# Attention in one kernel with a mixture of experts: the values' shared block kept twice, and transposed-weight buffers of the width of their half

## The chip, the cores and the metric

The kernel runs on one core of a Trainium2 chip. The metric is the device time in microseconds (us); lower is better. Before the change the median of three runs is 808.53 us (808.22 to 809.11).

## The reference, cut to what matters

Three layers follow each other: attention, a mixture of experts, and a feed-forward layer with a rational function. The change is in the attention, whose last line is the product of the weights and the values.

```python
B, H, S, D = q.shape                      # 2, 8, 576, 64
scores = (1 / np.sqrt(D)) * np.matmul(q, k.transpose(0, 1, 3, 2))
scores = scores + bias.transpose(2, 0, 1)[None]          # a small network of positions
attn = np.exp(scores - scores.max(-1, keepdims=True))
attn = attn / (attn.sum(-1, keepdims=True) + 1e-09)
attn_out = np.matmul(attn, v)             # the change is here
x = moe(attn_out)                         # 4 experts, 1152 tokens, 512 -> 1024 -> 512
out = rational_ffn(x)                     # 512 -> 2048 -> 512
```

## The kernel before, in words

The work runs in four stages: the bias of the positions (to about 62 us), attention (to about 217 us), the experts, and the rational layer. There is one instruction queue for each engine. TensorE is PE, VectorE DVE, ScalarE ACT, GpSimd POOL; SyncE (SP) issues nearly all transfers. In the attention stage a small planner, class `Flow`, writes the order of the instructions: each step has an assumed duration and an urgency from a table (`CFG`), and the order comes out of these alone. The change touches neither the durations nor the table.

Attention goes over eight passes n, one for each batch and pair of heads; the two heads of a pair are worked on together. A head has 576 keys, which is four and a half blocks of 128. The two halves share the ninth block: chunk 4 of the values' tile `splv` holds the last 64 keys of head 0 in partitions 0 to 63 and the first 64 keys of head 1 in partitions 64 to 127. The transposed weights lie in the same way: `pt` holds four full blocks for each head, `pe` the shared block.

Precision is kept by splitting numbers in a high and a low part: `splv` holds both side by side (128 columns), and the weights come as `pth`/`peh` (high) and `ptl`/`pel` (low).

The steps of a pass:

- `load_raw` (L517) fetches k, q and v of a pass; `split_hi` and `split_lo` (L527, L532, on POOL) split them; `qk_T` (L548, L556) transposes q and k; `swap_k` (L561) copies k with its halves swapped.
- `scores` (L594, PE), `biased` (L608, DVE), `exps` (L616, ACT), `norm` (L636, POOL).
- `transp` and `transp_rest` (L653, L666, L669, PE) transpose the normalized weights; ACT writes the high part (L678), DVE the low part (L682).
- `av` (L701, PE) multiplies with the values, once for each half of the queries (256 or 320 of them) and each head: ten matmuls, of which the first eight use 128 rows of the array. The last two, for the shared block, use the 64 rows of the head in question. A pass has four such runs of ten, so the kernel has 32.
- `other_half` (L708, ACT), `add_halves` (L714, DVE) and `x_parts` (L721, L722, POOL) bring the result to the experts' input `x`.

In the bias stage ACT makes a quarter of the hidden layers (L413) and all the results `bo` (L442). Four results share a buffer; there are two buffers, and each is stored to DRAM by SP (L431). The ninth result can't be written before the first buffer has been stored. During this stage SP also loads k, q and v of passes 0 and 1 and then eight small tables (`ab`, `dp`, L198 to L207), all in one queue.

Of the kernel before, what the change touches and what calls it, by code (L numbers as in the profile page):

```python
# [9 lines left out]
F32 = mybir.dt.float32  # L10
F32R = mybir.dt.float32r
# [7 lines left out]
B, H, S, D, HID = 2, 8, 576, 64, 32  # L19
# [5 lines left out]
P = 128  # L25
# [109 lines left out]
class Kernel:  # L135
# [366 lines left out]
    def load_raw(self, n, nm):  # L502

        if n >= 8:
            return
        nc = self.nc
        p, b = n // 2, n % 2
        src = self.t[nm][b, 2 * p:2 * p + 2]  # L510
        r = self.front.tile([P, 9, D], F32, tag="raw" + nm, bufs=1, name="raw" + nm)
        if nm == "q":
            for h in range(2):
                nc.sync.dma_start(out=r[:, 4 * h:4 * h + 4], in_=src[h, 0:512].rearrange("(c p) d -> p c d", p=P))
                nc.sync.dma_start(out=r[64 * h:64 * h + 64, 8], in_=src[h, 512:S].rearrange("(a q) d -> q a d", a=4))
        else:
            nc.sync.dma_start(out=r, in_=src.rearrange("h s d -> (h s) d").rearrange("(c p) d -> p c d", p=P))  # L517
        self.raw[n, nm] = r
# [4 lines left out]

    def split_hi(self, n, nm):
        nc, raw = self.nc, self.raw[n, nm]
        s = self.front.tile([P, 9, 2, D], F32R, tag="spl" + nm, bufs=(2 if nm == "v" else 1), name="spl" + nm)
        nc.gpsimd.tensor_scalar(out=s[:, :, 0, :], in0=raw, scalar1=1.0, scalar2=1.0, op0=ALU.mult, op1=ALU.mult)  # L527
        self.spl[n, nm] = s

# [35 lines left out]
    def attention_setup(self):  # L565

        nc, early = self.nc, self.early
# [69 lines left out]

        def pt_tiles(n, half):
            if (n, half) not in PT:
                PT[n, half] = tuple(  # L640
                    (self.att.tile([P, 4, 2, 320], F32R, tag="pt" + x, bufs=2, name="pt" + x),
                     self.att.tile([P, 320], F32R, tag="pe" + x, bufs=2, name="pe" + x)) for x in "hl")
            return PT[n, half]

        def transp(g):

            n, c, h = where(g)
            (mh, eh), (ml, el) = pt_tiles(n, 0 if c < 2 else 1)
            pt = Pt[n, c]
            o = P * (c % 2) if c < 4 else 256  # L650
            ps = self.one().rearrange("p (e i) -> p e i", e=4)
            for e in range(4):
                nc.tensor.transpose(ps[:, e, :], pt[:, 640 * h + e * P:640 * h + e * P + P], self.ident)  # L653
            if c < 4:
                todo = [(ps, mh[:, :, h, o:o + P], ml[:, :, h, o:o + P])]
            else:
                todo = [(ps.rearrange("p e (h q) -> p e h q", h=2), mh[:, :, :, 256:320], ml[:, :, :, 256:320])]
            parts[g] = (todo, [])

        def transp_rest(g):  # L660
            n, c, h = where(g)
            (mh, eh), (ml, el) = pt_tiles(n, 0 if c < 2 else 1)
            ps = self.one()
            if c < 4:
                for i in range(2):
                    nc.tensor.transpose(ps[:, P * i:P * i + P], Pt.pop((n, c - 1 + i))[:, 512:640], self.ident)  # L666
                rest = [(ps[:, 0:256], eh[:, 0:256], el[:, 0:256])]
            else:
                nc.tensor.transpose(ps[:, 0:P], Pt.pop((n, c))[:, 512:640], self.ident)  # L669
                rs = [slice(64 * hh, 64 * hh + 64) for hh in range(2)]  # L670
                rest = [(ps[r, r], eh[r, 256:320], el[r, 256:320]) for r in rs]
            parts[g] = (parts[g][0], rest)
# [14 lines left out]
        def av(n, half, h, part):  # L687
            W = 256 if half == 0 else 320
            vs = self.spl[n, "v"]
            (mh, eh), (ml, el) = PT[n, half]  # L690
            if part == 0:
                avs[n, half, h] = self.one()
            ps = avs[n, half, h]
            for e in ((0, 1), (2, 3, 4))[part]:
                for (m, el_) in ((mh, eh), (ml, el)):
                    if e < 4:
                        lh, rh = vs[:, 5 * h + e].rearrange("p a d -> p (a d)"), m[:, e, h, :W]
                    else:
                        r = slice(64 * h, 64 * h + 64)
                        lh, rh = vs[r, 4].rearrange("p a d -> p (a d)"), el_[r, :W]  # L700
                    nc.tensor.matmul(ps[:, :W], lhsT=lh, rhs=rh, start=(e == 0 and m is mh), stop=(e == 4 and m is ml))  # L701

        def other_half(n, half, h):
# [36 lines left out]
        def schedule():  # L740
# [54 lines left out]
            for n in range(8):  # L795
                p_hold = {}
                for r in range(9):
# [36 lines left out]
                    if r in (3, 8):  # L834
                        gs = range(9 * n, 9 * n + 4) if r == 3 else range(9 * n + 4, 9 * n + 9)
                        deps = [split_op[n, "v"]] + [Lop[x] for x in gs] + [Lop2[x] for x in gs if x in Lop2]
                        pre = None
                        xt = fl.hold("xt", 1)
                        adds = []
                        for h in range(2):  # L840
                            one = fl.hold("one", 4)
                            for part in range(2):
                                dur = (.48, .71)[part] if r == 3 else (.59, .88)[part]
                                lastav = h == 1 and part == 1
                                pre = fl.op("PE", dur, g + off("V", n), lambda n=n, half=half, h=h, part=part: av(n, half, h, part), deps if pre is None else [pre],
                                            take=[one] if part == 0 else [], free=[pt_hold[n, half]] if lastav else [])
                            go = fl.op("ACT", .385, g + off("G", n), lambda n=n, half=half, h=h: other_half(n, half, h), [pre] + adds, take=[xt] if h == 0 else [])
                            adds.append(fl.op("DVE", .41, g + off("G", n) + .1, lambda n=n, half=half, h=h: add_halves(n, half, h), [go], free=[one]))
                        avop.setdefault(n, []).append(pre)
                        xp[n, half] = fl.op("POOL", (1.2, 1.4)[half], g + off("X", n), lambda n=n, half=half: x_parts(n, half), adds, free=[xt])  # L850
# [433 lines left out]
```

## Time and profile before

The page describes one profiled execution.

| what | value |
|---|---|
| profiled execution, its own time | 807.95 us |
| its span, first to last instruction | 806.0 us |
| median of three runs | 808.53 us |
| PE busy | 783.1 us (97%) |
| DVE busy | 649.4 us (81%) |
| ACT busy | 488.3 us (61%) |
| POOL busy | 455.0 us (56%) |
| granted TensorE clock | 0.999 of full speed |

The engine with the largest share is PE. Shares are means over four stages with different limits, so a stage is read by itself: its stretch in the table of busy times, the chain of waits through it, and the instructions in order of time. A matmul's duration in the trace is longer than the distance between two matmuls, because they are pipelined; so costs of matmuls are read from the distances between their starts.

### The profile page before, as it was taken

The numbers are of one execution on the slowest core, as the hardware profiler recorded it, in microseconds if no ns is written. First come the engines' busy times: TensorE is split into PE (matmuls) and PEld (weight loads), VectorE is DVE, ScalarE is ACT, GpSimd is POOL, SyncE is SP. The second block draws the span as 40 slices with busy tenths as digits, with TensorE's granted clock in tenths as the row PEclk, the third lists the DMA queues.
The fourth block names the chain that finished last, engine by engine and source line by source line (L and its number), as shares of the span: only waits on it lengthen the run. The fifth ranks groups of instructions, "written<-read, shape, count | busy, mean of one in ns | idle before, by whom it ended". The sixth has DMA issues, their size and how long they took to land.

```text
span 806.0 us, 13644 instructions
## 1 busy us (share of the span) xinstructions
PE 783.1 (97%) x4980; PEld 683.0 (85%) x4980; DVE 649.4 (81%) x1183; ACT 488.3 (61%) x932; POOL 455.0 (56%) x454
## 2 busy tenths in 40 slices
PE   6888999999999999999999999999999999999997
PEld 2337899988998999999999999999889889998986
DVE  7987888888687888878889878888678667888775
ACT  5898898889443334333333433333369998887772
POOL 3167689778346555444355545345166977754442
PEclk9999999999999999999999999999999999999999
DMA  5788747491013434432444333333130311000012
GB/s 127 264 284 229 196 104 201 105 233 54 1 30 102 131 131 129 137 116 93 147 139 144 131 105 119 117 131 105 40 105 27 119 64 53 1 0 1 1 40 78
DMA packets 67634, 87.37 MB, mean 108 GB/s; under 512 B 33520, under 2 KB 42096, under 8 KB 67440
## 3 DMA queue, kind: packets, MB, share of 16 engines
q1 hardware_dynamic: 66992, 86.35, 35.4%
q8 instruction: 39, 0.64, 0.3%
q14 instruction: 27, 0.22, 0.1%
q10 hardware_dynamic: 576, 0.16, 0.1%
HBM read 60.12 MB, written 21.36 MB: 101 GB/s over the span
## 4 chain that ended last, share of the span: by engine, by line
PE 77%; ACT 7%; POOL 6%; issue 4%; DVE 4%; DMA 2%; SPq 0%; POOLq 0%; DVEq 0%; ACTq 0%
PE ps_o L900 20%; PE ps_o L1150 11%; PE ps_y L992 10%; PE ps_h L1142 10%; PE ps_x L992 8%; PE ps L701 6%; PE ps L594 5%; PE ps L653 4%; ACT hid L413 2%; ACT bo L442 2%; POOL we L303 2%; PE ps_x L890 1%; PE ps L548 1%; POOL wml L303 1%; PE ps_y L890 1%
## 5 line engine op out<-in xcount | busy, mean ns | idle before, releaser
L900 PE MATMUL ps_o<-we,hs 128*128 128x512 f32 x810 | 203.4, 392 | 0.0
L900 PEld LDWEIGHTS ps_o<-we,hs 128*128 128x128 f32 x810 | 146.1, 188 | 25.8
L303 POOL TENSOR_TENSOR we<-wstg,we 128x512 fp32r<-128x512 f32 x40 | 57.0, 1446 | 130.3 <-ACT we L297 130.3
L906 DVE SCALAR_TENSOR_TENSOR acc<-ps_o,prob,acc 128x512 f32<-128x512 f32 x135 | 99.7, 743 | 30.1 <-PE ps_o L900 29.9
L1123 POOL TENSOR_TENSOR qq<-qq,ha 128x384 f32<-128x384 f32 x48 | 48.9, 1019 | 71.0 <-ACT qq L1120 71.0
L1150 PE MATMUL ps_o<-wmh,hs 128*128 128x512 f32 x252 | 83.5, 392 | 1.1 <-POOL hs L1134 1.1
L1142 PE MATMUL ps_h<-x,wmh 128*128 128x384 f32 x288 | 73.7, 337 | 0.0
L636 POOL TENSOR_SCALAR P<-P,ri 128x576 f32<-128x576 f32 x72 | 53.0, 747 | 33.3 <-DVE ri L627 18.8
L930 ACT ACTIVATE hs<-ps_x 128x576 fp32r<-128x576 f32 x32 | 20.8, 651 | 80.7 <-DVE ps_x L1004 74.0
L608 DVE CUSTOM_DVE_ANT_0 P<-ps,bias 128x576 f32<-128x576 f32 x72 | 53.6, 750 | 14.9 <-PE ps L594 12.9
L424 PE MATMUL ps_ab<-hid,wm 128*32 128x288 f32 x576 | 47.0, 425 | 12.0 <-DVE hid L416 7.5
L616 ACT ACTIVATE P<-P,nm 128x576 f32<-128x576 f32 x72 | 56.0, 780 | 3.3 <-DVE nm L608 3.1
L1129 DVE SCALAR_TENSOR_TENSOR qq<-qq,rr 128x384 f32<-128x384 f32 x48 | 26.6, 554 | 38.1 <-ACT rr L1128 35.1
L1150 PEld LDWEIGHTS ps_o<-wmh,hs 128*128 128x128 f32 x252 | 47.3, 188 | 11.4 <-POOL hs L1134 1.9
L328 POOL TENSOR_TENSOR wu<-wt,wu 128x512 fp32r<-128x512 f32 x28 | 36.2, 1314 | 36.4 <-ACT wu L324 36.4
L1142 PEld LDWEIGHTS ps_h<-x,wmh 128*128 128x128 f32 x288 | 52.6, 188 | 2.0
L682 DVE TENSOR_TENSOR ptl<-ps,pth 128x512 fp32r<-128x512 f32 x72 | 48.5, 683 | 5.2 <-ACT pth L678 4.7
L416 DVE TENSOR_SCALAR hid<-ltab,shift 128x576 f32<-128x576 f32 x108 | 52.6, 558 | 0.0
L594 PE MATMUL ps<-kh,qs 128*128 128x288 f32 x168 | 50.3, 321 | 1.4 <-DVE nm L608 1.3
L1134 POOL TENSOR_TENSOR hs<-pp,hs 128x384 fp32r<-128x384 f32 x48 | 48.9, 1019 | 3.5 <-issue 2.8
L424 PEld LDWEIGHTS ps_ab<-hid,wm 128*32 128x32 f32 x576 | 18.4, 112 | 37.0 <-ACT bo L442 13.9
L1150 PE MATMUL ps_o<-wml,hs 128*128 128x512 f32 x126 | 49.5, 393 | 0.0
(142 smaller groups left out, 2098.9 us busy)
## 6 DMA issues: line engine op xcount, KB each, us to landing
wstg<-moe_w SPq DMA_DIRECT2D x32, 512.0 KB, 3.7
bias_d<-bo SPq DMA_DIRECT2D x9, 1152.0 KB, 5.4
bias<-bias_d SPq DMA_DIRECT2D x16, 576.0 KB, 5.1
w<-moe_w_in SPq DMA_DIRECT2D x16, 512.0 KB, 4.4
w<-moe_w_out SPq DMA_DIRECT2D x16, 512.0 KB, 3.8
kl<-kh SPq DMA_DIRECT2D x16, 288.0 KB, 4.4
w_u<-wmag SPq DMA_DIRECT2D x16, 256.0 KB, 2.4
w_d<-wmag SPq DMA_DIRECT2D x16, 256.0 KB, 2.4
```

What stands on the lines that cost most here:

```text
L303: nc.gpsimd.tensor_tensor(out=lo[:, sl], in0=stg[:, sl], in1=hi[:, sl].bitcast(F32), op=ALU.subtract)
L416: eng.tensor_scalar(out=ht, in0=d, scalar1=c, scalar2=0.0, op0=ALU.add, op1=ALU.max)
L424: nc.tensor.matmul(ps[32 * q:32 * q + 32, i, 0:288], lhsT=wm, rhs=hs[q][:, 288 * i:288 * i + 288], start=True, stop=True)
L594: nc.tensor.matmul(ps[:, half, dst:dst + w], lhsT=lhs, rhs=k[:, src:src + w], start=(i == 0), stop=(i == len(m) - 1))
L608: nc.vector.tensor_tensor_reduce(out=Pt[u][:, S * h:S * h + S].rearrange("p (a b) -> p a b", a=2), in0=ps[:, :, 0:288], in1=self.bias_t[n ...
L616: nc.scalar.activation(out=pt, in_=pt, func=AF.Exp, scale=-1.0, bias=stat.pop(g), accum_out=sums[n, c][:, h:h + 1])
L636: nc.gpsimd.tensor_scalar(out=pt[:, sl], in0=pt[:, sl], scalar1=ri, scalar2=1.0, op0=ALU.mult, op1=ALU.mult)
L900: nc.tensor.matmul(ps, lhsT=a, rhs=w[:, f, :], start=(f == i == 0), stop=(f == 1 and i == 2))
L906: nc.vector.scalar_tensor_tensor(out=acc[:, t], in0=ps, scalar=pr, in1=acc[:, t], op0=ALU.mult, op1=ALU.add)
L992: nc.tensor.matmul(ps[:, half, 0:288], lhsT=wu[:, w, i, k], rhs=x[v][:, k, 288 * half:288 * half + 288], start=(start and k == j == 0), st ...
L1142: nc.tensor.matmul(ps, lhsT=w[:, k, fo:fo + P], rhs=v[:, k, :], start=(k == i == 0), stop=(k == 3 and i == 2))
L1150: nc.tensor.matmul(ps, lhsT=a[:, P * tt:P * tt + P], rhs=w[:, f % 2, :], start=(f == i == 0), stop=(f == 3 and i == 2))
```

## The change

The raw values of a pass now have ten chunks instead of nine. Chunk 4 holds the last 64 keys of head 0, and zeros in the other 64 partitions; the new chunk 9 holds the first 64 keys of head 1, and zeros in the others. One buffer `rawv` is made in the first pass, its zeros are written once by POOL, and all passes load into it. A load of v is four transfers instead of one. The split works on ten chunks. The two matmuls of the shared block then take all 128 rows: the zeros remove the other head's keys. The transposed weights of each half of the queries get a buffer of their own with the width of that half, one of each, in place of two of the larger width.

```diff
+        if nm == "v":
+            if n == 0:
+                self.rawv = self.front.tile([P, 10, D], F32, tag="rawv", bufs=1, name="rawv")
+                for h in range(2):
+                    nc.gpsimd.memset(self.rawv[64 - 64 * h:128 - 64 * h, 4 + 5 * h], 0.0)
+            r = self.rawv
+            rows = src.rearrange("h s d -> (h s) d").rearrange("(c p) d -> p c d", p=P)
+            for h in range(2):
+                nc.sync.dma_start(out=r[:, 5 * h:5 * h + 4], in_=rows[:, 5 * h:5 * h + 4])
+                nc.sync.dma_start(out=r[64 * h:64 * h + 64, 4 + 5 * h], in_=rows[64 * h:64 * h + 64, 4])
+            self.raw[n, nm] = r
+            return
...
-        s = self.front.tile([P, 9, 2, D], F32R, tag="spl" + nm, bufs=(2 if nm == "v" else 1), name="spl" + nm)
+        s = self.front.tile([P, 9 + (nm == "v"), 2, D], F32R, tag="spl" + nm, bufs=(2 if nm == "v" else 1), name="spl" + nm)
...
+                W = (256, 320)[half]
                 PT[n, half] = tuple(
-                    (self.att.tile([P, 4, 2, 320], F32R, tag="pt" + x, bufs=2, name="pt" + x),
-                     self.att.tile([P, 320], F32R, tag="pe" + x, bufs=2, name="pe" + x)) for x in "hl")
+                    (self.att.tile([P, 4, 2, W], F32R, tag=f"pt{x}{half}", bufs=1, name="pt" + x),
+                     self.att.tile([P, W], F32R, tag=f"pe{x}{half}", bufs=1, name="pe" + x)) for x in "hl")
...
-                    if e < 4:
-                        lh, rh = vs[:, 5 * h + e].rearrange("p a d -> p (a d)"), m[:, e, h, :W]
-                    else:
-                        r = slice(64 * h, 64 * h + 64)
-                        lh, rh = vs[r, 4].rearrange("p a d -> p (a d)"), el_[r, :W]
+                    lh, rh = vs[:, 5 * h + e].rearrange("p a d -> p (a d)"), m[:, e, h, :W] if e < 4 else el_[:, :W]
                     nc.tensor.matmul(ps[:, :W], lhsT=lh, rhs=rh, start=(e == 0 and m is mh), stop=(e == 4 and m is ml))
```

The order on PE, DVE and ACT is that of before, instruction for instruction. SP's queue grows by three transfers in each of the eight loads of v. The first place is in the bias stage: the load of v for pass 1 (`rawv`), the small tables (`ab`, `dp`), and then the first stores of the bias (`bias_d`). Before:

```order
14 L515 DMA rawq<-q 64x1x64
15 L517 DMA rawv<-v 128x9x64
16 L198 DMA ab<-moe_a 128x4
17 L199 DMA ab<-moe_b 128x2
18 L207 DMA dp<-moe_domain_probs 128x4x4
19 L207 DMA dp<-moe_domain_probs 128x3x4
20 L207 DMA dp<-moe_domain_probs 64x4 x2
21 L207 DMA dp<-moe_domain_probs 64x1x4 x2
22 L431 DMA bias_d_71<-bo 128x4x576 x2
```

The same place of SP's queue with the change:

```order
17 L528 DMA rawq<-q 64x1x64
18 L520 DMA rawv<-v 128x4x64
19 L521 DMA rawv<-v 64x64
20 L520 DMA rawv<-v 128x4x64
21 L521 DMA rawv<-v 64x64
22 L198 DMA ab<-moe_a 128x4
23 L199 DMA ab<-moe_b 128x2
24 L207 DMA dp<-moe_domain_probs 128x4x4
25 L207 DMA dp<-moe_domain_probs 128x3x4
26 L207 DMA dp<-moe_domain_probs 64x4 x2
27 L207 DMA dp<-moe_domain_probs 64x1x4 x2
28 L431 DMA bias_d_71<-bo 128x4x576 x2
```

The first store of the bias stands three transfers later in the same queue. The second place is on SP in the attention stage, the copy of k (`kl`) and the load of v for pass 6, ahead of q for pass 7. Before:

```order
94 L561 DMA kl<-kh 64x1152
95 L562 DMA kl<-kh 64x1152
96 L517 DMA rawv<-v 128x9x64
97 L514 DMA rawq<-q 128x4x64
98 L515 DMA rawq<-q 64x1x64
```

The same place of SP's queue with the change:

```order
112 L574 DMA kl<-kh 64x1152
113 L575 DMA kl<-kh 64x1152
114 L520 DMA rawv<-v 128x4x64
115 L521 DMA rawv<-v 64x64
116 L520 DMA rawv<-v 128x4x64
117 L521 DMA rawv<-v 64x64
118 L527 DMA rawq<-q 128x4x64
119 L528 DMA rawq<-q 64x1x64
```

The load of q, which POOL splits, stands three transfers later.

## Rows read from the trace of the kernel before

**Rows 1.** The page, busy time of PE (us, share, instructions)
```profile
PE 783.1 (97%) x4980; PEld 683.0 (85%) x4980; DVE 649.4 (81%) x1183; ACT 488.3 (61%) x932; POOL 455.0 (56%) x454
```
**Rows 2.** Busy times of a stretch of the attention: us, PE, PEld, DVE, ACT, POOL, clock, DMA
```profile
87.00:180.70 93.70, 92.95 (x703) 84.63 (x701) 78.64 (x246) 83.14 (x207) 77.72 (x105) 1.00 0.66 169
```
**Rows 3.** Chain of waits, bias stage and attention: start us, us, what
```profile
57.96 0.64 ACT bo L442
...
80.34 0.76 POOL P L636
...
82.00 0.80 PE ps L594 x4
```
**Rows 4.** PE in order of time, 256 queries: start us, us, engine, line, tiles, shapes
```profile
133.40 0.29 PE L594 MATMUL ps<-kl,qs 128*128 128x288 f32 x1
133.53 0.28 PE L701 MATMUL ps<-pth,splv 128*128 128x256 f32 x1
...
134.35 0.28 PE L701 MATMUL ps<-ptl,splv 128*128 128x256 f32 x1
134.56 0.38 PE L701 MATMUL ps<-peh,splv 64*128 64x256 f32 x1
134.79 0.27 PE L701 MATMUL ps<-pel,splv 64*128 64x256 f32 x1
134.99 0.40 PE L594 MATMUL ps<-kh,qs 128*128 128x288 f32 x1
135.23 0.29 PE L594 MATMUL ps<-kl,qs 128*128 128x288 f32 x1
```
**Rows 5.** PE in order of time, 320 queries
```profile
105.60 0.31 PE L701 MATMUL ps<-ptl,splv 128*128 128x320 f32 x1
...
106.48 0.31 PE L701 MATMUL ps<-ptl,splv 128*128 128x320 f32 x1
106.72 0.41 PE L701 MATMUL ps<-peh,splv 64*128 64x320 f32 x1
...
107.46 0.30 PE L701 MATMUL ps<-ptl,splv 128*128 128x320 f32 x1
```
**Rows 6.** Groups by line and shape: count, busy us, mean ns
```profile
L701 PE MATMUL ps<-peh,splv 64*128 64x320 f32 x16 | 6.6, 411 | 0.0
L701 PE MATMUL ps<-peh,splv 64*128 64x256 f32 x16 | 6.1, 382 | 0.0
```
**Rows 7.** Weight loads in order of time, at the run of rows 5
```profile
106.34 0.19 PEld L701 LDWEIGHTS ps<-ptl,splv 128*128 128x128 f32 x1
106.72 0.18 PEld L701 LDWEIGHTS ps<-peh,splv 64*128 64x128 f32 x1 [0.19 <-ACT qs L556]
```
**Rows 8.** Waits of ACT, 82 to 200 us: total us, times, longest
```profile
ACT xt L708 <- PE ps L701: 6.2, 13, 0.9
```
**Rows 9.** Issues of SP in the bias stage: start us, us, line, tiles
```profile
13.77 0.55 SPq L515 DMA_DIRECT2D rawq<-q  x1
14.53 0.41 SPq L517 DMA_DIRECT2D rawv<-v  x1
14.98 0.60 SPq L198 DMA_DIRECT2D ab<-moe_a  x1
...
19.65 1.45 SPq L431 DMA_DIRECT2D bias_d<-bo  x1
```
**Rows 10.** ACT in order of time, bias stage
```profile
25.71 0.74 ACT L442 ACTIVATE bo<-ps_ab,rpsi 128x576 f32<-128x576 f32 x1 [2.58 <-DMA bias_d<-bo]
```
**Rows 11.** Groups by line and shape, POOL's split of v
```profile
L532 POOL TENSOR_TENSOR splv<-rawv,splv 128x576 fp32r<-128x576 f32 x8 | 11.5, 1435 | 0.2
L527 POOL TENSOR_SCALAR splv<-rawv 128x576 fp32r<-128x576 f32 x8 | 5.6, 702 | 0.0
```
**Rows 12.** SP's issue of the v of pass 6
```profile
158.90 0.72 SPq L517 DMA_DIRECT2D rawv<-v  x1
```
**Rows 13.** POOL in order of time, split of the q of pass 7
```profile
166.90 0.67 POOL L527 TENSOR_SCALAR splq<-rawq 128x576 fp32r<-128x576 f32 x1 [0.16 <-issue]
```

## The prediction, made before the changed kernel had run

> **What bounds the kernel now.** I read the shares of the engines first: PE is busy for 97% of the span, no other engine over 81% [rows 1]. That is a mean, so next came the stretch the change lies in. From 87.0 to 180.7 us, five of the eight attention passes, PE is busy 92.95 of 93.70 us, ACT 83.14, DVE 78.64, POOL 77.72 [rows 2]. So PE is the bound there, and ACT is second with 10.56 us free. The chain of waits says the same from the other side: until about 82 us it still runs through POOL, from 82.00 us on it is almost all PE [rows 3]. A busy share does not say that PE works well, though, so I then read the starts of the matmuls in order of time.
>
> In a run of ten with 256 queries, the eight matmuls on 128 rows start 0.117 us apart: 134.35 − 133.53 = 0.82 over seven steps [rows 4]. Then the distances grow: 0.21 to the first 64-row matmul, 0.23 to the second, 0.20 to the next instruction (again on 128 rows) and 0.24 to the one behind. With 320 queries the clean distance is (106.48 − 105.60)/6 = 0.147, and the same four steps take 107.46 − 106.48 = 0.98 us [rows 5]. The reader is to see that the two narrow matmuls, which do half the work, are late on their way in and on their way out.
>
> **The change part by part.**
>
> *The 64-row pair goes.* Without late starts the four steps would take 3 × 0.117 + 0.135 = 0.49 us with 256 queries (0.135 is the distance of the scores' matmuls, 288 wide, 0.13 between the last two ahead of the run [rows 4]) and 4 × 0.147 = 0.59 with 320. They take 0.88 and 0.98, so a pair costs 0.39 us in either width. There are 16 + 16 pairs [rows 6]. Where transposes follow instead of wide matmuls (13 of the 32, counted in the chain) I see only some 0.3 us, as the last of the four steps is hardly late: 19 × 0.39 + 13 × 0.32 = 11.6 us. The replacement runs over 128 rows with the same number of columns, so I take 0.117 and 0.147 us for it, the distance of its eight neighbours. What is taken away lies on the bounding engine, except in the first run, near 77 us, where the chain goes through POOL [rows 3]: 2 pairs, 0.78 us, cost nothing now and give nothing back. That leaves 10.8 us.
>
> The row on weight loads shows how it is lost: a normal load starts while the matmul before it still runs (106.34), but the load of the 64-row block begins at 106.72, the same moment as its matmul, after 0.19 us without a load [rows 7]. The Trainium skill, "TensorEngine Tiling (Array Packing)", section "Key Properties", says that changing the tiling mode empties the engine first. It would put the cost on the two changes, (0.09 + 0.08) × 32 = 5.4 us by this case's distances; the trace has all four steps late, so the sum stands by the trace.
>
> *What else has to keep up.* PE would gain 10.8 us over the eight passes less most of the first, say 7.2, so 1.5 us a pass. ACT has 10.56/5 = 2.1 us a pass free, so it would run at 96 to 97%. It fits, but queues in fixed order at this load lose something. For it: what ACT waits for most is this same product, 6.2 of its waits [rows 8], so ACT gains from the cure as well. I take 85% of 10.8: 9.2 us. Bounds: the 6.2 us alone, if ACT's other waits stay, and the full 10.8.
>
> *Three more transfers in each load of v.* In the bias stage SP is the late one. SP issues v of pass 1 at 14.53, the small tables from 14.98, and the first store of the bias at 19.65 without a pause in between [rows 9], so SP's queue and not ACT sets when that store leaves. The store lands, and ACT, which had to wait for it for 2.58 us, goes on at 25.71 [rows 10]. From there ACT sets the pace until 58.6 us, in the chain of waits [rows 3]. So what is added ahead of that store is on the path: three issues at 0.55 + 0.04 = 0.59 us, 1.77 us, and POOL's longer split of v of pass 0, for which the load of pass 1 waits: (0.702 + 1.435)/9 = 0.24 us [rows 11]. That makes 2.0 us. Bounds: nothing, if the store lands sooner after its issue than now, and 2.6 if the small pieces also slow the transfers behind them. I take 2.0, since the issue slots are measured. The Trainium skill, "DMA: Bandwidth & Descriptors", section "Rules for kernel authors", advises against it too: transfers to disjoint halves of the partitions should be one, many small ones should be joined. It has no price for SP's queue, and the sum goes by SP's rows.
>
> In the attention stage the loads of v have a pass or so of slack themselves. What stands behind them in SP's queue has less: the q of pass 7, issued after the v at 158.90 [rows 12], is split by POOL at 166.90 after a short wait of 0.16 us [rows 13]; it will be some 1.8 us late, and POOL's split with it. The transposes that need POOL's next results come more than 2 us after those, so I put 0.2 us for it, bounds 0 and 1.8.
>
> *Rest.* POOL's split of v grows by 0.24 us in six passes; POOL has 16 us free in rows 2, so 0. The two fills of zeros lie at the start, where POOL waits for input: 0. The narrower weight buffers are used in the same rotation, one for each half: 0; bounds ±0.5, since addresses move.
>
> **Sum.** −9.2 + 2.0 + 0.2 = −7.0 us on the profiled execution's 807.95 us (span 806.0): 800.95. The median of the runs is 0.58 above it, so 801.5 us.
>
> **The rivals.**
> 1. *ACT takes over.* PE's freed time turns into waits for ACT and DVE, and only the 6.2 us go. For it: ACT at 97% in a fixed order. Against: its free time is more than is needed. −6.2 + 2.2 = −4.0: 804.5.
> 2. *Everything is realized, and the bias stage loses nothing.* −10.8 + 0.2: 797.9. For it: PE's chain without gaps. Against: SP's unbroken row of issues ahead of the store.
> 3. *The late starts stay.* The pair might be late since it changes operands (`pe` for `pt`), not rows. The Trainium skill, "TensorE: Matmul & The Clock Gate", section "Step-by-step: what each phase is for", says that a weight load is pulled ahead of running matmuls when its row groups don't conflict or it goes to the background buffer; by it the 64-row load should not be late at all, and something else would have to be the cause. As a mechanism of this kernel: the change of operands costs, and remains. Against it: from the scores to the first product, other weights and other operands, the distance is 0.13 us, no delay [rows 4]. Result: 2.2 us slower, 810.7.
> 4. *SP's queue becomes the bound: slower.* Each of the six later loads of v holds up q, k or the bias behind it by 2.0 us, and POOL or DVE miss them. 2.0 + 6 × 2.0 − 10.8 = +3.2: 811.7. It decides from the fifth such load on, as 2.0 + 2.0 n passes 10.8 at n = 4.4. For it: the wait in rows 13. Against: the engines' rows show but that one such wait.
>
> **How the numbers follow.** My forecast, with gains of 9 to 5 us (799.5 to 803.5): 0.50. Rival 1 (803.5 to 806.9): 0.20. Rival 2 (below 799.5): 0.17. Rival 3: 0.07. Rival 4: 0.03. Gain and loss balancing: 0.03. About 0.2%, 1.6 us, is what a measurement of this kernel can tell from no change; so faster 0.87, same 0.03, slower 0.10. The range goes from the lower end of rival 2, 797.5, into rival 1, 805.8; that leaves out rivals 3 and 4, the balance and the worst of rival 1, together under 0.2. The forecast's own range is 799.5 to 803.5.
>
> **What would show it.** In the changed profile the ten matmuls of a run should start evenly, 0.117 or 0.147 us apart, and no weight load begin with its own matmul there. The first store of the bias should be issued near 21.7 us, and ACT's wait for it grow from 2.58 to about 4.6. ACT's waits for the product should shrink to below half. From the end of the attention on all stages should keep their length. I am wrong if the last two matmuls of a run stay late, if PE gets new waits for ACT, DVE or POOL of over 4 us in the attention, or if the bias stage ends at its old time.

## The result, and the profile after

The median of three runs of the changed kernel is 801.25 us (801.18 to 801.47), against 808.53 before: a ratio of 0.9909, interval 0.9894 to 0.9923. The forecast was 801.5. The profiled execution took 801.47 us (span 799.6), 6.5 less than that of before.

The page's busy times, to set beside [rows 1]:

```profile
PE 774.1 (97%) x4980; PEld 682.6 (85%) x4980; DVE 649.4 (81%) x1183; ACT 488.9 (61%) x932; POOL 445.3 (56%) x456
```

PE does the same 4980 matmuls in 9.0 us less. Five passes by the table of busy times, answering to [rows 2]:

```profile
87.00:180.70 93.70, 91.45 (x749) 89.42 (x748) 83.61 (x263) 88.96 (x220) 82.68 (x110) 1.00 0.67 173
```

In equal time PE now gets through 749 instructions instead of 703. ACT is at 95% and PE, at 98%, still ahead of it. PE in order of time, 256 queries, is what answers to [rows 4]:

```profile
131.92 0.30 PE L607 MATMUL ps<-kl,qs 128*128 128x288 f32 x1
132.05 0.28 PE L711 MATMUL ps<-pth,splv 128*128 128x256 f32 x1
...
132.88 0.28 PE L711 MATMUL ps<-ptl,splv 128*128 128x256 f32 x1
132.99 0.28 PE L711 MATMUL ps<-peh,splv 128*128 128x256 f32 x1
133.11 0.28 PE L711 MATMUL ps<-pel,splv 128*128 128x256 f32 x1
133.23 0.29 PE L607 MATMUL ps<-kh,qs 128*128 128x288 f32 x1
133.36 0.29 PE L607 MATMUL ps<-kl,qs 128*128 128x288 f32 x1
```

From the eighth matmul to the second instruction behind the run it is now 133.36 − 132.88 = 0.48 us, where [rows 4] had 0.88. The weight loads in a run with 320 queries, as in [rows 7]:

```profile
158.77 0.19 PEld L711 LDWEIGHTS ps<-ptl,splv 128*128 128x128 f32 x1
158.92 0.19 PEld L711 LDWEIGHTS ps<-peh,splv 128*128 128x128 f32 x1
159.06 0.19 PEld L711 LDWEIGHTS ps<-pel,splv 128*128 128x128 f32 x1
```

They follow each other every 0.15 us, those of the shared block as the others. ACT's wait for the product, 6.2 us in [rows 8], is small (82 to 195 us):

```profile
ACT xt L718 <- PE ps L711: 1.7, 6, 0.5
```

The price stands in the bias stage. SP's issues, from the v of pass 1 to the first store (compare [rows 9]):

```profile
14.68 0.38 SPq L520 DMA_DIRECT2D rawv<-v  x1
15.10 0.51 SPq L521 DMA_DIRECT2D rawv<-v  x1
...
16.85 0.58 SPq L198 DMA_DIRECT2D ab<-moe_a  x1
...
20.16 1.22 SPq L207 DMA_DIRECT2D dp<-moe_domain_probs  x1
...
22.11 0.53 SPq L431 DMA_DIRECT2D bias_d<-bo  x1
```

ACT's wait for that store ([rows 10]):

```profile
27.05 0.74 ACT L442 ACTIVATE bo<-ps_ab,rpsi 128x576 f32<-128x576 f32 x1 [3.35 <-DMA bias_d<-bo]
```

The store is issued 2.46 us later, but from its issue to ACT's going on it is 27.05 − 22.11 = 4.94 us instead of 6.06, so ACT loses 1.34. Most of that difference is SP's own time for the issue, 1.45 us in [rows 9] and 0.53 here; from the end of the issue to ACT's going on it is 4.61 us before and 4.41 after. A long issue now stands at one of the small tables instead (1.22 us, at 20.16).

Last, POOL's split of the q of pass 7 ([rows 13]), and the group of its waits:

```profile
164.11 0.68 POOL L540 TENSOR_SCALAR splq<-rawq 128x576 fp32r<-128x576 f32 x1 [0.94 <-DMA rawq<-q]
```

To find where time goes I set the same instruction's start in both traces side by side. The first product stands at 76.47 us before and 79.15 after; two lines show the other end, the first matmul of the experts, before and after:

```profile
218.26 2.01 PE L890 MATMUL ps_x<-x,we 128*128 128x288 f32 x14
```
```profile
212.03 3.46 PE L900 MATMUL ps_x<-x,we 128*128 128x288 f32 x24
```

| point | before | after | difference |
|---|---|---|---|
| last product of the bias stage | 61.24 | 62.60 | +1.36 |
| first product with the values | 76.47 | 79.15 | +2.68 |
| pass 1 | 95.97 | 97.63 | +1.66 |
| pass 5, its second run | 172.95 | 168.10 | −4.85 |
| pass 5, its third run | 180.67 | 176.60 | −4.07 |
| experts' first matmul | 218.26 | 212.03 | −6.23 |
| span | 805.95 | 799.62 | −6.33 |

The reader is to see three things: a loss of 1.36 in the bias stage; a further 1.3 us lost from 62.6 to 79.2 that no term of the forecast holds; and a gain of 8.9 us from there to the experts, in which 0.8 is given back at pass 5. That unforeseen 1.3 is a fall of TensorE's granted clock. The table of busy times there (clock third from the end), and PE's rows:

```profile
66.20:69.70 3.50, 3.50 (x19) 3.48 (x19) 1.30 (x3) 1.81 (x5) 3.50 (x5) 0.51 0.84 258
```
```profile
66.12 0.96 PE L561 MATMUL ps<-identr,splk 128*128 128x128 f32 x6 [2.17 <-ACT bo L442]
...
67.25 0.44 PE L607 MATMUL ps<-kl,qs 128*128 128x288 f32 x1
67.49 0.44 PE L607 MATMUL ps<-kh,qs 128*128 128x288 f32 x1
...
69.85 0.29 PE L607 MATMUL ps<-kl,qs 128*128 128x288 f32 x1
69.98 0.29 PE L607 MATMUL ps<-kh,qs 128*128 128x288 f32 x1
```

After a wait of 2.17 us for ACT the scores' matmuls start 0.24 us apart, at 1.2 GHz, until 69.63; then 0.13, at 2.4 GHz. The trace of before has the same wait of 2.17 us, and no fall:

```profile
64.76 0.71 PE L548 MATMUL ps<-identr,splk 128*128 128x128 f32 x6 [2.17 <-ACT bo L442]
...
65.51 0.29 PE L594 MATMUL ps<-kl,qs 128*128 128x288 f32 x1
65.64 0.29 PE L594 MATMUL ps<-kh,qs 128*128 128x288 f32 x1
```

Whether the change brings it was open.

### The profile page after: what moved, and what is told of

Same layout as the page of the kernel before. It is cut to its first block, busy times and chain, and to the rows that moved or that the text cites. A ratio compares the mean times of both kernels' runs of the same rounds, so it can differ in the third digit from the quotient of the medians.

```text
span 799.6 us, 13676 instructions
## 1 busy us (share of the span) xinstructions
PE 774.1 (97%) x4980; PEld 682.6 (85%) x4980; DVE 649.4 (81%) x1183; ACT 488.9 (61%) x932; POOL 445.3 (56%) x456
## 4 chain that ended last, share of the span: by engine, by line
PE 78%; ACT 10%; POOL 5%; DVE 4%; issue 2%; DMA 1%; SPq 0%; POOLq 0%; DVEq 0%; ACTq 0%
PE ps_o L910 23%; PE ps_y L1002 11%; PE ps_o L1160 10%; PE ps_h L1152 9%; PE ps_x L1002 8%; PE ps L607 4%; PE ps L711 4%; PE ps L667 3%; ACT bo L442 2%; ACT hid L413 2%; ACT P L629 1%; POOL wml L303 1%; PE ps_x L900 1%; PE ps L561 1%; POOL we L303 1%
```

## The experiments

The ratios are against runs of the kernel before on the same chip (medians 807.97 and 807.98 in the first two sessions, 807.59 and 808.25 beside e9 and e10).

**e1, the loads alone.** The changed kernel, with the 64-row pair as before:

```diff
+                    if e < 4:
+                        lh, rh = vs[:, 5 * h + e]..., m[:, e, h, :W]
+                    else:
+                        r = slice(64 * h, 64 * h + 64)
+                        lh, rh = vs[r, 4 + 5 * h]..., el_[r, :W]
```

> The changed kernel's loads, split and buffers, but the two matmuls of the shared block on 64 rows as before (the right half of chunks 4 and 9). Theory A (the gain is the 64-row pair's late starts, the loads cost): slower than before by 1.3 us, ACT's longer wait for the first bias store, or by up to 2.7 us if the TensorE clock falls once near 66 us as it did with the change: 809.8 to 811.2 us. All 32 pairs keep their late starts of 0.39 us. Rival B (buffers and loads bring the gain): 801 to 805 us.

810.19 us, ratio 1.0027 (1.0017 to 1.0037): the loads cost, and pay nothing. The bias stage ends 1.63 us late, ACT's wait for the store is 3.9 us. The first product comes 2.89 us late; the 1.3 in between are the fall again (its clock is at 1.2 GHz from 66.3 to 69.7). From there to the end the distance stays at 2.8 to 2.9, so six later loads of v cost nothing while the product is slow, and ACT's wait for the product is the old 6.2.

**e2, the wide pair alone.** The kernel before, with two slices changed:

```diff
-                        lh, rh = vs[r, 4]..., el_[r, :W]
+                        lh, rh = vs[:, 4]..., el_[:, :W]
```

> The kernel before, with all 128 rows for the two matmuls of the shared block; the other head's 64 keys are left in the sum instead of zeros, nothing else differs. Theory A: the ten matmuls of a run start evenly, 0.117 and 0.147 us apart, ACT's wait for the first bias store stays 2.58 us, and the time falls by 8.9 us (what the changed kernel gained between its first product and the end of the attention) to 10.8 us: 797.7 to 799.6 us. Rival B (the pair is late since its operands change): 808.5 us, the pairs still late.

798.30 us, 0.9878 (0.9865 to 0.9892). PE with 320 queries:

```profile
121.63 0.31 PE L700 MATMUL ps<-ptl,splv 128*128 128x320 f32 x1
121.78 0.31 PE L700 MATMUL ps<-peh,splv 128*128 128x320 f32 x1
121.92 0.31 PE L700 MATMUL ps<-pel,splv 128*128 128x320 f32 x1
122.07 0.31 PE L700 MATMUL ps<-pth,splv 128*128 128x320 f32 x1
```

Same operands, same order, and the delay is gone: it belongs to the number of rows. From the start of the first run of ten to the start of the last the gain is 9.6 us; the later experiments are compared by the same measure. By the medians e1 loses 2.2 us and e2 gains 9.7, together −7.5, where the change has −7.3.

**e4, the small tables behind the first store.** The changed kernel, with the tables' loads two steps later:

```diff
-            if gg == 3:
+            if gg == 5:
                 self.setup_const()
```

> The changed kernel, with the small tables (ab, dp) issued behind the first bias store instead of ahead of it. Theory A (SP's queue delays the store, ACT waits for it): the store is issued near 18 us instead of 22.1, ACT's wait of 3.35 us falls under 0.5, and the bias stage ends some 3 us sooner: 798.0 to 798.6 us; 1.3 us less still if the TensorE clock no longer falls near 66 us. Rival (the store's landing is set by the transfers in flight, not by its issue): within 0.5 us of 801.25.

798.59 us, 0.9883 (0.9868 to 0.9898). The store's issue:

```profile
17.66 0.38 SPq L431 DMA_DIRECT2D bias_d<-bo  x1
```

ACT has no wait for it any more, and the bias stage ends at 59.81, 2.8 us sooner than in the changed kernel: the loss of that stage was SP's queue. Pass 5 still gives back 0.85 us, with POOL's wait for the q of pass 7 at 1.02.

**e5, the same in the kernel before.**

> The kernel before, with the small tables (ab, dp) issued behind the first bias store. Theory A (SP's queue, not the change's loads, set when the store left in the kernel before as well): ACT's wait of 2.58 us is gone, the bias stage ends 1.5 to 2.6 us sooner, the time is 1.5 to 2.6 us below that of the kernel before on the same chip. Rival (the store waits for something else): within 0.5 us of the kernel before.

806.59 us, 0.9983 (0.9975 to 0.9992): 1.4 us, short of the least expected. The bias stage ends 1.73 us sooner, as theory A has it, but the first product only 0.60, since the profiled execution has the fall of the clock:

```profile
64.20:67.60 3.40, 3.40 (x16) 3.38 (x16) 1.98 (x5) 2.33 (x6) 3.40 (x5) 0.50 0.94 209
```

So the fall also comes in a kernel without the change.

**e6, PE kept busy in its wait.** The changed kernel with 24 matmuls, whose results nobody reads, at the end of the bias stage:

```diff
+        ps = self.ps.tile([P, 2, 512], F32, tag="ab", bufs=3, name="ps_ab")
+        for i in range(6):
+            for q in range(4):
+                nc.tensor.matmul(ps[32 * q:32 * q + 32, i % 2, 0:288], lhsT=wm, rhs=hids[:, q, 0:288], start=True, stop=True)
```

> The changed kernel, with 24 more matmuls at the end of the bias stage, into a spare bank that nothing reads, so that PE works through most of its wait of 2.2 us at 64 us. Theory A (that wait lets the TensorE clock fall to 1.2 GHz from 66.2 to 69.6 us, which costs 1.3 us): no stretch at 1.2 GHz there, the first product of pass 0 starts some 1.3 us sooner than 79.15, the time is 799.6 to 800.2 us. Rival (the fall belongs to something else in the stretch): the stretch stays, or moves, and the time is 801.0 to 801.6 us.

800.52 us, 0.9906 (0.9890 to 0.9921). In its profile the clock does not fall, but the first product comes at 79.00, only 0.15 sooner: the added matmuls run until 66.5 and take what the clock gives. Inconclusive on the price of the fall. The profile shows something else, though: e6 has the changed kernel's attention unaltered, yet POOL does not wait for the q of pass 7, pass 5 gives nothing back, and the attention gains 9.4 us, where the changed kernel gains 8.4.

```profile
162.93 0.68 POOL L544 TENSOR_SCALAR splq<-rawq 128x576 fp32r<-128x576 f32 x1
```

SP spends 0.55 to 0.59 us on each of the four issues of that q here; in the changed kernel's profile one of the four takes 1.19.

**e10, the changed kernel again.** After e5 and e6 I looked at the mean granted clock of every single execution, and put the question to the unaltered kernel.

> The changed kernel itself, unaltered, executed more often. What it tells apart: whether the fall of TensorE's granted clock near 66 us in its profile belongs to the kernel or to the single execution. The kernel before, in the 34 executions beside the earlier experiments, had a mean granted clock of 0.999 in 16, with 806.56 to 807.98 us, and of 0.997 to 0.998 in 18, with 807.97 to 809.48; the profiled execution had 0.999 and no fall, the changed kernel's 0.998 and one fall. Theory A (each execution has the fall or not, whatever the kernel, and it costs about 1.1 us): the changed kernel's executions fall into two groups as well, 0.999 with 799.7 to 800.5 us and 0.996 to 0.998 with 800.8 to 801.8. Theory B (the changed bias stage brings the fall): all of them have 0.998 or less and 800.8 to 801.8 us, none 0.999.

(The count in it is off by one: 17 and 17 of the 34.) Four executions: 800.04 and 800.46 us with a clock of 1.000, 801.09 and 801.36 with 0.997. That is theory A; B falls. The profiled one is that with 800.04; the same stretch of PE, same wait, no fall:

```profile
65.90 0.71 PE L561 MATMUL ps<-identr,splk 128*128 128x128 f32 x6 [2.17 <-ACT bo L442]
66.44 0.36 PE L607 MATMUL ps<-kh,qs 128*128 128x288 f32 x1
66.65 0.29 PE L607 MATMUL ps<-kl,qs 128*128 128x288 f32 x1
66.77 0.29 PE L607 MATMUL ps<-kh,qs 128*128 128x288 f32 x1
```

Its bias stage ends 1.14 us late, its first product stands at 77.60 (+1.13), so nothing is lost in between, and the experts begin at 210.47:

```profile
210.47 1.74 PE L900 MATMUL ps_x<-x,we 128*128 128x288 f32 x11
```

That is −7.79 against before, the span 798.2 against 805.95. With the 7 runs beside this one the kernel before has 41 executions with a known clock: 19 at 0.999 with a median of 807.52 us, 22 at 0.997 or 0.998 with 808.73. Read so, about half of the executions have a fall, and it costs about 1 us in either kernel. For executions without a profile the mean is a sign and no proof, since it also counts the end of the span: e4's profile has 0.998 without such a fall, as its last 2.44 us, in which no engine computes, are at 1.2 GHz.

**e7, two raw buffers.** e4 with two buffers for the raw v, so that v is loaded a pass earlier and q stands ahead of it:

```diff
-                self.rawv = ...(bufs=1)
+                self.rawv = [...(bufs=2) for _ in range(2)]
...
+            if gg == 7:
+                self.load_v(2)
```

> The kernel with the tables later, with two buffers for the raw v, each loaded a pass earlier, and the loads of v for passes 5 and 7 issued behind the q that follows them in SP's queue. Order on PE, DVE, ACT and POOL unchanged. Theory A (the q of pass 7 comes late because the four transfers of v stand ahead of it; that cost 0.9 to 1.2 us near 171 us): POOL's wait for that q falls from 0.9 us to 0, the time is 0.8 to 1.3 us below that of the kernel with the tables later alone: 797.3 to 797.8 us. Rival (from pass 5 on ACT is full, and the time would be lost later): within 0.4 us of 798.59.

800.63 us, 0.9906 (0.9892 to 0.9921): a miss. I had put the load of pass 2 ahead of the second store of the bias, and repeated the fault that e4 had mended:

```profile
33.61 0.74 ACT L443 ACTIVATE bo<-ps_ab,rpsi 128x576 f32<-128x576 f32 x1 [3.61 <-DMA bias_d<-bo]
```

The bias stage ends 2.29 us late, and the first product comes 3.34 late, with the clock at 1.2 GHz from 68.5 to 71.9. From the first run of ten to the last, though, this kernel gains 9.4 us where e4 gains 8.4, and POOL's wait for q is gone.

**e9, that load behind the store.** e7 with `gg == 9` in place of `gg == 7`.

> The kernel of e7_two_raw_buffers with one change: the load of v of pass 2 is issued at step 9 of the bias stage instead of step 7, so behind the second store of the bias in SP's queue instead of ahead of it. Theory A (the second raw buffer saves the late q of pass 7, and e7 lost its time only since that load stood ahead of a store): ACT's wait of 3.6 us for the store goes, the bias stage ends at e4_tables_later's -1.4 us against before, and the attention gains e7's 9.4 us from the first product on instead of e4's 8.4: 798.59 less 0.8 to 1.3, so 797.3 to 797.8. POOL's wait for q of pass 7 (1.02 us in e4) is gone. Theory B (the gain of e7 in the attention was only the lateness of its bias stage being caught up): the attention gains 8.4 as in e4, 798.4 to 798.8. A fall of the granted clock between 62 and 72 us, which some of these kernels show and others not, would put either 0.9 to 1.3 us higher.

798.20 us (796.53 to 798.77), 0.9878 (0.9858 to 0.9898). ACT does not wait, the bias stage ends at −1.48, the attention gains 9.4 by the same measure, POOL does not wait for q: theory A in each step, except that e6 had the same gain without the second buffer, so that the buffer brings it is not shown. The profiled execution, 797.83 us, has the fall, right at the attention's start:

```profile
63.48:66.88 3.40, 3.40 (x19) 3.38 (x18) 1.36 (x3) 1.76 (x5) 3.40 (x5) 0.50 0.83 256
```

The one of its four executions with a clock of 0.999 is the one with 796.53. The intervals of e9 and e4 overlap, so which of the two is faster is not shown; both are faster than the changed kernel (their slowest executions took 798.77 and 798.86 us, the fastest of its seven 800.04).

**e3, the two heads' pairs together.** The kernel before, in which the second head takes its shared block first, right behind the first head's:

```diff
+            seq = (0, 1, 2, 3, 4) if h == 0 else (4, 0, 1, 2, 3)
+            for e in ((seq[:2], seq[2:]) if h == 0 else (seq[:3], seq[3:]))[part]:
```

> The kernel before, with the 64-row pair of head 1 first in its run of ten, so that in 12 of 16 places it stands right behind the pair of head 0 (rows 0 to 63, then rows 64 to 127). Theory A1 (changing between 128 and 64 rows costs): one entry and one exit go in 12 places, 12 x 0.39 = 4.7 us, less what the first one on the POOL chain hides: 804.0 to 804.8 us. Theory A2 (each 64-row matmul is late by itself, or a change of half costs as much as a change of mode): 807.5 to 808.5 us, with late starts inside the four.

802.66 us, 0.9931 (0.9919 to 0.9944): more than either theory had.

```profile
105.29 0.31 PE L702 MATMUL ps<-ptl,splv 128*128 128x320 f32 x1
105.53 0.42 PE L702 MATMUL ps<-peh,splv 64*128 64x320 f32 x2
105.78 0.31 PE L702 MATMUL ps<-pel,splv 64*128 64x320 f32 x2
106.02 0.42 PE L702 MATMUL ps<-pth,splv 128*128 128x320 f32 x1
```

Each narrow row now holds two matmuls (x2), one for each head, in the time of one. One head's lie in rows 0 to 63 of the array, the other's in 64 to 127.

**e8, both pairs on the same rows.** e3 with `r = slice(0, 64)` for both heads.

> The kernel with the two 64-row pairs together, but both on rows 0 to 63; head 1's first 64 keys are replaced by head 0's last. Theory A (in that kernel the pairs of the two heads run at the same time since they use different halves of the rows): now they run one after the other, two more distances of 0.117 or 0.147 us in 11 places on the path, 2.6 to 3.2 us slower than 802.66: 805.2 to 805.9 us. Rival (the whole gain came from fewer changes between 128 and 64 rows): 802.3 to 803.0 us.

805.12 us, 0.9958 (0.9945 to 0.9972).

```profile
106.71 0.31 PE L702 MATMUL ps<-ptl,splv 128*128 128x320 f32 x1
106.95 0.41 PE L702 MATMUL ps<-peh,splv 64*128 64x320 f32 x1
107.20 0.30 PE L702 MATMUL ps<-pel,splv 64*128 64x320 f32 x1
107.35 0.31 PE L702 MATMUL ps<-peh,splv 64*128 64x320 f32 x1
107.49 0.30 PE L702 MATMUL ps<-pel,splv 64*128 64x320 f32 x1
107.73 0.42 PE L702 MATMUL ps<-pth,splv 128*128 128x320 f32 x1
```

Now they follow each other. From the last wide start to the next it is 1.02 us here and 0.73 in e3. In the attention e3 gains 5.85 us and e8 3.60, so 2.25 us of e3's gain is matmuls beside each other. The rows show the delay as well: 0.24 and 0.25 on the way in, 0.24 on the way out, but 0.15 and 0.14 between neighbours of 64 rows. It is the change between 64 and 128 rows that costs, not 64 rows in themselves.

## Why the prediction was right, step by step

The terms are best read from two executions without a fall of the clock, the profiled one of before and that of e10.

- **The pair's late starts.** Right as a mechanism: starts even at 0.117 and 0.147, no load at its own matmul's start, and e2 rules out rival 3. In size, 9.2 of 10.8 was a little low. From the first product (+1.13) to the experts (−7.79) it is 8.92 us, with 0.86 given back at pass 5, so 9.8; e9, without that loss, has 9.86. That is 91% and not 85%. e2, which changes nothing but the rows, gains 10.1 over the same stretch.
- **ACT keeps up.** Right. PE's gain was put at 1.5 us a pass; from pass 1 to pass 5 it is (4.46 + 1.66)/4 = 1.53. ACT is at 95%, not 96 to 97. PE's waits for other engines, from 82 us to the end of the attention, grow from 0.9 to 2.9 us, below the 4 us named as a sign of being wrong. Rival 1 falls.
- **Three more transfers ahead of the first store.** The mechanism is right (e4: with the tables moved the loss goes), the size was 2.0 and is 1.1 to 1.4. The store was to leave near 21.7 and left at 22.11, but came home 1.1 us quicker after its issue. I had named that as the lower bound and dropped it, taking the time from issue to landing as fixed; ACT's wait is 3.35, not 4.6. What I had taken for one time holds two: SP's own time for the issue, 1.45 us before and 0.53 after, and the transfer, which differs by 0.2 only. The three added issues cost what I had put (1.75 us, from 15.10 to 16.85), but the end of the store's issue moved by 1.54 us where its start moved by 2.46. Why single issues are long, these runs do not show.
- **The late q of pass 7.** Put at 0.2, measured 0.8 to 0.9 in both profiles of the changed kernel and in e4, and nothing in e6: the step that failed most. I had argued with more than 2 us of room behind POOL's split. In the chain of waits the stretch behind it no longer belongs to PE alone:

```profile
174.25 1.64 ACT P L629 x4
176.60 1.72 PE ps L711 x10
181.57 0.95 ACT we L297
...
192.99 1.48 POOL P L649 x2
```

  Once PE is quicker the room is smaller, and e6, e7 and e9 show that the loss goes with the wait. The same load under the slow product cost nothing, and POOL does not wait there (e1). The three transfers alone do not decide it, as e6 has them too: in the profiles with the wait one issue of q is long (1.19 us in the first, 1.71 in e10, 1.69 in e4), in e6 none is. That this issue makes the wait fits the lengths, but was not tested. The 0.16 us in [rows 13], which I had counted as a wait for q, the profile puts down to POOL's own issue.
- **The rest at nothing.** Right within 0.2: from the experts on all stages keep their length (−6.23 at their start, −6.33 at the end).

The sum: −9.8 + 1.1 + 0.9 = −7.8 without falls, where −7.0 was forecast. What the sum didn't have, the fall near 66 us, put 1.3 us on the one profiled execution. The median of 808.53 was hardly free of falls itself: its three runs, from 808.22 up, lie where before has its executions with one, above all 19 without. So the medians differ by 7.3 us, nearer to the sum than the two profiled executions do with 6.5. That the forecast met the median within 0.3 us owes something to errors of opposite sign: the product mis-sized by 0.6 and the bias by 0.6 to 0.9 on one side, q by 0.7 on the other.

Rival 2 was right about the product (nearly all is realized) and wrong on the bias. Rival 4 saw the right place, but of the six later loads of v one held something up, and not in every execution.

## What to carry to other kernels

A matmul on half of the rows between matmuls on all rows costs more than its work: look at the distances of starts, not at durations, and fill the missing rows with zeros where the operand can be kept so. Count what such a fix adds to the queues ahead of the first store somebody waits for, and order the queue by who waits; that was worth another 2.2 to 2.7 us here (e4 against the two medians of the changed kernel). And before a difference of 1 us between two profiles is explained, look at the granted clock of both.

## What the runs showed of the hardware that was not expected

Matmuls on rows 0 to 63 and on rows 64 to 127 that stand next to each other ran at the same time (e3: two in 0.25 us, where e8 needs 0.15 for each one more). The Trainium skill, "TensorEngine Tiling (Array Packing)", section "Key Properties", states that tiles load and multiply in parallel; the trace agrees, and my expectation for e3 had left it out.

The clock's fall to 1.2 GHz after a wait of 2.17 us comes in one execution and not in the next of the same program: the changed kernel has it in the first profile and not in the second. The Trainium skill, "TensorE: Matmul & The Clock Gate", section "What's actually happening", calls the slow stretch at a kernel's start run-variable; here it is in the middle of one. What decides it in a given execution these runs don't show. The matmuls added in e6 leave its profile without a fall, but gain no time, and two of its four executions have a mean clock of 0.997.

SP's time for one issue is not constant: most take 0.4 to 0.6 us, but single ones 1.2 to 2.0 (the first store in [rows 9] 1.45, one of q in e10 1.71, one of v in e9 2.01), and in the bias stage the long one fell on the store before the change and on a table after it.
